# Convolution by a Winograd-like transform: order of work in the second unit, of the first unit's outer silu, and the engines of a few adds

## The chip, the cores and the metric

The kernel runs on one core of a Trainium2 chip. A core has a matrix engine (TensorE, PE in the profile), a vector engine (VectorE, DVE), a scalar engine (ScalarE, ACT), GpSimd (POOL), and an engine that mostly issues transfers (SyncE, SP). Each works through its own instructions in order and waits for the others on semaphores. TensorE writes only to PSUM, a memory of eight banks. The metric is device time in microseconds (us); lower is better.

## The reference

```python
y = sum(jnp.einsum('bsc,cd->bsd', xp[:, k:k + S, :], w[k]) for k in range(3))
y = (y - mean) * (g / sqrt(var + 1e-5)) + b
return silu(y)
```

This is a convolution of width 3 along the sequence (`xp` is `x` with one row of zeros at either end), a normalization by channel with given statistics, and a silu. Inputs and output are bfloat16; `x` is 2 x 2048 x 1024, `w` is 3 x 1024 x 1024.

## The kernel before, in words

The convolution is not made tap by tap. Six output rows at a time are computed from eight transformed inputs and eight transformed weights (a transform of Winograd's kind, with points 0, 1, -1, 2, -2, 1/2, -1/2 and infinity). There are 342 such blocks of six rows in each of the two batches.

The inputs are transformed on TensorE (`t_job`, L305 to L326): a matmul of windows of `x` with a small matrix, then a cast from PSUM to the tile `T_sb[bi]` on ScalarE or VectorE. Each cast goes to the engine that a small model of the engines' clocks, kept in Python while the program is written, says would end it first (`busy` and `ends` add to those clocks).

The weights are transformed for one block of 128 output channels (`dc`, 0 to 7) at a time. Taps 0 and 7 are the raw `w0` and `w2`. The six others come in three pairs, q = 0, 1, 2: a sum `e` (q = 0: `w0 + w2`; q = 1: `4 w2 + w0`; q = 2: `4 w0 + w2`), to which the middle tap (`w1`, or `2 w1` for q = 1 and 2) is added, or from which it is subtracted (`transform_w`, L184 to L190, on GpSimd: two instructions for a pair). The tiles are called `u0`, `u1`, `u2`. Where a sum needs four times a tap, VectorE does it in one instruction (L171), or another engine first writes the multiple to a scratch tile `w1x2` (two buffers) and GpSimd adds (L169, L249). There is one buffer for each of `e0`, `e1`, `e2`, and there are two for each of `u0`, `u1`, `u2`.

The main work goes by units: one block of channels and one batch, 15 whole units and a last one in two halves. Units take PSUM banks 0 to 3 and 4 to 7 in turn. A unit consists of eight products; a product (`product(q, j, ...)`, L351) is eight matmuls that add up over the input channels into one bank, q, of the unit. The order in a unit after the first (`run`, L465) is

```python
product(3,1); copy; product(0,3); copy; product(3,2); copy; product(0,4)
product(2,5); copy; product(2,6)   # then the previous unit's rest between
```

ScalarE copies a partial product away (`copy`, L366), and the next product adds into the same bank. VectorE combines banks and copies to the six output rows (`combine`, L376). Rows 0 and 5 lie in the unit's banks 0 and 3, rows 1 and 4 in banks 1 and 2, rows 2 and 3 in an SBUF tile `t1`. The two outer products, (0,0) with tap 0 for row 0 and (3,7) with tap 7 for row 5, are left for the next unit: `rest` (L457) returns pairs of a number and a function, and `run` calls those of number n at its point n (`behind(n)`; 1 to 4 stand behind the first four products, 5 behind the copy of (2,5), 6 at the end). In the usual order, `rest(between, 5, 6)`, the inner silus (`silu_inner`) and (3,7) with the silu of row 5 come at point 5, and (0,0) with the silu of row 0 at point 6. The silu (L380) reads PSUM or `t1` and writes `yT`. SyncE then transposes `yT` and stores it.

The first unit (`run_first`, L407) is different: its outer products come first and are copied to a tile `ends`, and the jobs that transform the second batch's inputs are put between its products. GpSimd adds `ends` to `t0` and `t2` (L435, L436), so nothing is left for later but the silus: `rest_first` (L450) puts the inner ones at point 5 and the outer ones, one instruction for both rows, at point 6 of the second unit. The weights of the second block of channels are made within the first two units by `prepare_second` (L232): `first` in the middle of the first unit, `times4` and the VectorE sum at its end, and `second` at point 1 of the second unit.

All instructions stay on each engine in the order in which the program issues them.

Of the kernel before, what the change touches and what calls it, by code (L numbers as in the profile page):

```python
# [9 lines left out]
ALU = mybir.AluOpType  # L10
# [5 lines left out]
P = 128  # L16
# [10 lines left out]
def kernel(  # L27
# [87 lines left out]
    def busy(e, size):  # L115
        clock[e] = ends(e, size)
# [115 lines left out]
    def prepare_second(dc):  # L232


        w0, w2 = raw[dc][:, 0], raw[dc][:, 2]
        g = spool.tile([P, CT, P], BF16, name="w1x2")

        def first():
            even_part(dc, 0, nc.gpsimd)
            transform_w(dc, 0, (0,))  # L240

        def times4():
            nc.scalar.mul(g, w2, 4.0)
            busy("act", CT * P)

        def second():
            double_w(dc, nc.scalar)
            sums[dc, 1] = epool.tile([P, CT, P], FP32, name="e1")
            nc.gpsimd.tensor_tensor(sums[dc, 1], g, w0, op=ALU.add)  # L249
            transform_w(dc, 1)  # L250
            transform_w(dc, 2)

        return first, times4, lambda: even_part(dc, 2, nc.vector), second

    prm = consts.tile([P, 4, DC], BF16, name="prm")
    scale = consts.tile([P, DC], FP32, name="scale")
# [78 lines left out]
    class Unit:  # L335
# [71 lines left out]
        def run_first(self, between, left, following):  # L407


            b0, b1, b2, b3 = self.bank  # L410
            sd = dpool.tile([P, 2, NB], FP32, name="sd")
            t0 = dpool.tile([P, 2, NB], FP32, name="t0")
            t2 = dpool.tile([P, 2, NB], FP32, name="t2")
# [12 lines left out]
            self.product(3, 2, True, between)  # L426
            self.copy(3, dst=sd[:, 0])
            self.combine(sd[:, 1], pa, 2.0, b3, ALU.subtract)
            self.product(0, 4, True, between)
            self.combine(b1, b0, -2.0, pb)  # L430
            for t, a in ((t0, -0.0125), (t2, -0.2), (t1, -0.05)):
                self.combine(t, self.low, a, sd)
            dc, (first, times4, third, second) = following
            first()
            nc.gpsimd.tensor_tensor(t0[:, 0], t0[:, 0], ends[:, 0], op=ALU.add)  # L435
            nc.gpsimd.tensor_tensor(t2[:, 1], t2[:, 1], ends[:, 1], op=ALU.add)  # L436
            transform_w(dc, 0, (1,))
            self.product(2, 5, False, between)
            pc = self.copy(2)
            between.rest()  # L440
            self.product(2, 6, True, between)
            self.combine(b3, b2, -0.5, pc)
            self.combine(self.low, self.high, -1.6, t0)
            self.combine(t1, self.high, -0.4, t1)
            self.combine(self.high, self.high, -0.1, t2)
            times4()
            third()
            self.second = second

        def rest_first(self):  # L450

            return [
                (1, self.second), (5, self.silu_inner),
                (6, lambda: self.silu(slice(0, R, R - 1), ps[:, self.b0:self.b0 + 4:3, self.lo:self.hi])),
            ]

        def rest(self, between, last=5, first=6):  # L457
# [4 lines left out]
                (first, lambda: self.first(between)),  # L462
            ]

        def run(self, between, also=(), prepare=None):  # L465
# [11 lines left out]
            t0 = dpool.tile([P, 2, NB], FP32, name="t0")[:, :, sl]  # L477
            t2 = dpool.tile([P, 2, NB], FP32, name="t2")[:, :, sl]
            self.y23 = t1 = ypool2.tile([P, 2, NB], FP32, name="t1")[:, :, sl]
            self.product(3, 1, False, between)  # L480
            pa = self.copy(3)
            behind(1)
            self.product(0, 3, False, between)
            pb = self.copy(0, by=4.0)
            behind(2)
            self.product(3, 2, True, between)
            self.copy(3, dst=sd[:, 0])
            self.combine(sd[:, 1], pa, 2.0, b3, ALU.subtract)
            behind(3)
            self.product(0, 4, True, between)  # L490
            behind(4)
            self.combine(b1, b0, -2.0, pb)
            for t, a in ((t0, -0.0125), (t1, -0.05), (t2, -0.2)):
                self.combine(t, self.low, a, sd)
            idle(dve_work)
            if prepare:
                prepare_w(prepare)
            self.product(2, 5, False, between)
            pc = self.copy(2)
            behind(5)  # L500
            self.product(2, 6, True, between)
            self.combine(b3, b2, -0.5, pc)
# [117 lines left out]
    for i, (dc, bi) in enumerate(seq[:-1]):  # L620
        unit = Unit(dc, bi, i % 2 * 4)
        if i == 0:
            unit.run_first(between, left[0], (1, prepare_second(1)))
# [67 lines left out]
```

## Time and profile before

| | |
|---|---|
| median of 3 runs | 190.01 us (190.00 to 190.02) |
| profiled execution | 190.22 us, span 188.5 us |
| TensorE busy | 177.0 us, 94% |
| VectorE busy | 154.2 us, 82% |
| GpSimd busy | 146.4 us, 78% |
| ScalarE busy | 111.0 us, 59% |

A row of a timeline has the start (us from the start of the span), the duration, the engine, the line of the kernel, the operation, what it writes and reads, the shapes, and how many instructions were merged into the row; in brackets stands how long the engine had been idle before and what released it. A row of waits has who waited for whom, then the total in us, the number of waits and the longest. A row of a group has the line, the shape and the count, then the busy time, the mean in ns and the idle time before. L359 is the matmul of the products, L370 and L372 are the copies, L377 is `combine`, L382 the silu. Durations of neighbouring instructions on one engine can overlap by about 0.1 us.

### The profile page before, as it was taken

The page shows a single profiled execution, that of the slowest core. Times are in us where ns is not written, and L with a number is a line of the kernel's source. Part 1 is how long each engine was busy: PE and PEld are TensorE (multiplying, and loading weights), DVE is VectorE, ACT ScalarE, POOL GpSimd, SP SyncE. Part 2 cuts the span into 40 slices and gives each one's busy share as a digit, 9 for nine tenths or more (in the row PEclk, how much of TensorE's full clock was granted, in tenths as well). Part 3 has the DMA queues.
Part 4 walks back from the last instruction along what each step waited for, and adds up shares of the span by engine and source line. Part 5 has one row for each costly group of instructions (what it writes and reads, how often), then busy time and mean ns, then how long its engine had stood idle before and what let it go on. Part 6 is the DMA issues. An engine that isn't in the chain of part 4 may idle for free.

```text
span 188.5 us, 3723 instructions
## 1 busy us (share of the span) xinstructions
PE 177.0 (94%) x1402; PEld 124.9 (66%) x1402; DVE 154.2 (82%) x213; ACT 111.0 (59%) x181; POOL 146.4 (78%) x87
## 2 busy tenths in 40 slices
PE   6769999998799999999999999999999999999981
PEld 2658688765466666666666666666666666669980
DVE  5548667899988999999877997799987996769781
ACT  3789698685547465456546563655455546364790
POOL 3468999979999779999999999899999972021022
PEclk9999999999999999999999999999999999999996
DMA  5999999057424839499669585996595766877835
GB/s 159 339 346 335 386 367 219 1 153 188 75 50 31 195 66 186 124 241 206 113 132 185 113 175 156 213 207 124 117 207 108 159 87 153 162 141 145 190 67 111
DMA packets 86958, 31.72 MB, mean 168 GB/s; under 512 B 73542, under 2 KB 82778, under 8 KB 86940
## 3 DMA queue, kind: packets, MB, share of 16 engines
q1 hardware_dynamic: 85820, 31.24, 72.4%
q10 hardware_dynamic: 864, 0.21, 0.5%
q8 instruction: 11, 0.18, 0.4%
q0 software_dynamic: 256, 0.03, 0.2%
q14 instruction: 7, 0.06, 0.1%
HBM read 14.82 MB, written 8.39 MB: 123 GB/s over the span
## 4 chain that ended last, share of the span: by engine, by line
PE 83%; DMA 5%; DVE 4%; ACT 3%; SPq 2%; issue 1%; DVEq 0%
PE ps L359 77%; PE ps L313 5%; DMA xw<-in_x_dram 5%; DVE T_sb L326 4%; SPq L125 2%; ACT yT L382 2%; ACT T_sb L324 1%; PE ps L521 1%; SPq L141 0%; DVEq L686 0%; ACT pc L370 0%; DVE sd L377 0%; DVE o L522 0%; DVEq L326 0%
## 5 line engine op out<-in xcount | busy, mean ns | idle before, releaser
L359 PE MATMUL ps<-T_sb,u 128*128 128x342 bf16 (+2 forms) x816 | 120.3, 299 | 1.7 <-ACT yT L382 1.2
L359 PEld LDWEIGHTS <-u 128*128 128x128 bf16 x816 | 76.7, 97 | 35.2 <-issue 2.1
L190 POOL TENSOR_TENSOR u<-e,w1x 128x1024 bf16<-128x1024 f32 x32 | 70.2, 2219 | 3.9 <-ACT sd L370 1.3
L359 PE MATMUL ps<-T_sb,wch 128*128 128x342 bf16 (+2 forms) x272 | 42.9, 299 | 0.5 <-ACT T_sb L324 0.5
L190 POOL TENSOR_TENSOR u<-e,wch 128x1024 bf16<-128x1024 f32 x16 | 38.7, 2435 | 1.8 <-DMA wch<-in_w_dram 1.2
L382 ACT ACTIVATE yT<-ps,beta,scale 128x342 bf16<-128x342 f32 (+4 forms) x49 | 33.6, 719 | 11.0 <-PE ps L359 10.9
L377 DVE SCALAR_TENSOR_TENSOR t<-ps,sd 128x684 f32<-128x684 f32 (+2 forms) x51 | 39.1, 821 | 0.6
L370 ACT COPY pc<-ps 128x342 f32<-128x342 f32 (+2 forms) x34 | 14.5, 427 | 33.8 <-PE ps L359 33.1
L359 PEld LDWEIGHTS <-wch 128*128 128x128 bf16 x272 | 25.6, 97 | 11.7 <-issue 0.7
L326 DVE CAST T_sb<-ps 128x1008 bf16<-128x1008 f32 (+2 forms) x20 | 22.1, 1121 | 11.8 <-PE ps L313 11.7
L324 ACT CAST T_sb<-ps 128x1008 bf16<-128x1008 f32 (+2 forms) x30 | 24.9, 866 | 7.2 <-PE ps L313 7.1
L377 DVE SCALAR_TENSOR_TENSOR ps<-ps,t 128x684 f32<-128x684 f32 (+2 forms) x34 | 28.3, 832 | 0.7
L313 PE MATMUL ps<-rm,xw 128*128 128x168 bf16 (+2 forms) x272 | 24.8, 233 | 3.1 <-DMA xw<-in_x_dram 2.6
L171 DVE SCALAR_TENSOR_TENSOR e<-wch 128x1024 f32<-128x1024 bf16 x13 | 26.7, 2051 | 0.0
L313 PEld LDWEIGHTS <-xw 128*128 128x128 bf16 (+2 forms) x272 | 20.1, 97 | 8.9 <-DMA xw<-in_x_dram 3.9
L377 DVE SCALAR_TENSOR_TENSOR ps<-ps,pc 128x342 f32<-128x342 f32 (+2 forms) x34 | 16.9, 496 | 7.8 <-PE ps L359 6.3
L169 POOL TENSOR_TENSOR e<-wch 128x1024 f32<-128x1024 bf16 x7 | 16.9, 2409 | 0.7 <-PE ps L359 0.7
L382 ACT ACTIVATE yT<-t,beta,scale 128x684 bf16<-128x684 f32 (+2 forms) x17 | 15.7, 926 | 0.0
L377 DVE SCALAR_TENSOR_TENSOR t<-ps,t 128x684 f32<-128x684 f32 (+2 forms) x17 | 13.9, 818 | 0.0
L377 DVE SCALAR_TENSOR_TENSOR sd<-pc,ps 128x342 f32<-128x342 f32 (+2 forms) x17 | 8.3, 486 | 6.8 <-ACT sd L370 6.7
L563 POOL DMA_DIRECT2D out_dram<-o x2 | 1.4, 712 | 15.6 <-DMA o<-yT 15.6
L370 ACT COPY sd<-ps 128x342 f32<-128x342 f32 (+2 forms) x17 | 7.3, 429 | 9.4 <-PE ps L359 9.2
(53 smaller groups left out, 57.9 us busy)
## 6 DMA issues: line engine op xcount, KB each, us to landing
xw<-in_x_dram SPq DMA_DIRECT2D x32, 256.0 KB
out_dram<-o SPq DMA_DIRECT2D x28, 192.0 KB
wch<-in_w_dram SPq DMA_DIRECT2D x9, 512.0 KB
out_dram<-o SPq DMA_DIRECT2D x14, 120.0 KB
wch<-in_w_dram SPq DMA_DIRECT2D x6, 256.0 KB
out_dram<-o SPq DMA_DIRECT2D x3, 128.0 KB
o<-yT SPq DMA_TRANSPOSE x15
out_dram<-o SPq DMA_DIRECT2D x12, 7.5 KB
```

The costliest lines, as they stand in the source:

```text
L125: nc.sync.dma_start(out=xw[0:hi - lo, :], in_=x[bi, lo:hi, :])
L169: eng.tensor_tensor(e, w0, w2, op=ALU.add)
L171: eng.scalar_tensor_tensor(out=e, in0=f, scalar=4.0, in1=h, op0=ALU.mult, op1=ALU.add)
L190: nc.gpsimd.tensor_tensor(wts[dc, q][:, i], sums[dc, q], o, op=(ALU.add, ALU.subtract)[i])
L313: nc.tensor.matmul(v[:, q, c], lhsT=xw[0:rows, (c0 + c) * P:(c0 + c + 1) * P], rhs=mat[0:rows, :, 0:n], start=True, stop=True,)
L324: nc.scalar.copy(dst, src)
L326: nc.vector.tensor_copy(dst, src)
L359: nc.tensor.matmul(self.bank[q], lhsT=lhsT, rhs=T_sb[self.bi][:, ct, j, nsl], start=not add and ct == 0, stop=ct == CT - 1, skip_group_che ...
L370: nc.scalar.copy(dst, self.bank[q])
L377: nc.vector.scalar_tensor_tensor(out=out, in0=in0, scalar=scalar, in1=in1, op0=ALU.mult, op1=op1)
L382: nc.scalar.activation(self.yT[:, rows, self.lo:self.hi], src, ACT.Silu, bias=beta[:, dc:dc + 1], scale=scale[:, dc:dc + 1])
L521: nc.tensor.transpose(v[:, a, q], self.yT[:, i, k * P:k * P + n], ident)
```

## The change

The change does six things.

- In the second unit alone (`alone`, i = 1), product (2,5) and its copy come ahead of product (0,4).
- The first unit's outer silu moves from point 6 to point 4 of the second unit, ahead of the inner silus, which stay at point 5.
- `ends` is added to `t0` and `t2` on VectorE, in one instruction over both: `t0` and `t2` become the halves of one tile `t02`. The instruction is also entered into the model of VectorE's clock. The two GpSimd adds go.
- All sums of the second block of channels are made on GpSimd: the q = 2 sum leaves VectorE, ScalarE writes 4 `w0` for it, and it is made behind the q = 1 pair.
- `prepare_second` is regrouped: both signs of `u0` are made one after the other; `4 w2` and the q = 1 sum come at the end of the first unit, `2 w1` and the `u1` pair at point 1 of the second, `4 w0`, the q = 2 sum and the `u2` pair at point 3.
- In the third unit (i = 2) the second unit's outer product (0,0) and its silu come at point 4 instead of point 6.

```diff
-        g = spool.tile([P, CT, P], BF16, name="w1x2")
+        def times4(tap):
+            t = spool.tile([P, CT, P], BF16, name="w1x2")
+            nc.scalar.mul(t, tap, 4.0)
+            busy("act", CT * P)
+            return t
+
+        def even(q, t, h):
+            sums[dc, q] = epool.tile([P, CT, P], FP32, name=f"e{q}")
+            nc.gpsimd.tensor_tensor(sums[dc, q], t, h, op=ALU.add)

         def first():
             even_part(dc, 0, nc.gpsimd)
-            transform_w(dc, 0, (0,))
-
-        def times4():
-            nc.scalar.mul(g, w2, 4.0)
-            busy("act", CT * P)
+            transform_w(dc, 0)

         def second():
+            even(1, times4(w2), w0)
+
+        def third():
             double_w(dc, nc.scalar)
-            sums[dc, 1] = epool.tile([P, CT, P], FP32, name="e1")
-            nc.gpsimd.tensor_tensor(sums[dc, 1], g, w0, op=ALU.add)
             transform_w(dc, 1)
+
+        def fourth():
+            even(2, times4(w0), w2)
             transform_w(dc, 2)

-        return first, times4, lambda: even_part(dc, 2, nc.vector), second
+        return first, second, third, fourth
...
-            for t, a in ((t0, -0.0125), (t2, -0.2), (t1, -0.05)):
-                self.combine(t, self.low, a, sd)
-            dc, (first, times4, third, second) = following
+            for d, a in ((t0, -0.0125), (t2, -0.2), (t1, -0.05)):
+                self.combine(d, self.low, a, sd)
+            nc.vector.tensor_tensor(t[:, 0::3], t[:, 0::3], ends, op=ALU.add)
+            busy("dve", 2 * NB)
+            first, second, third, fourth = following
             first()
-            nc.gpsimd.tensor_tensor(t0[:, 0], t0[:, 0], ends[:, 0], op=ALU.add)
-            nc.gpsimd.tensor_tensor(t2[:, 1], t2[:, 1], ends[:, 1], op=ALU.add)
-            transform_w(dc, 0, (1,))
             self.product(2, 5, False, between)
             pc = self.copy(2)
             between.rest()
...
-            times4()
-            third()
-            self.second = second
+            second()
+            self.prepare = third, fourth

         def rest_first(self):

             return [
-                (1, self.second), (5, self.silu_inner),
-                (6, lambda: self.silu(slice(0, R, R - 1), ps[:, self.b0:self.b0 + 4:3, self.lo:self.hi])),
+                (1, self.prepare[0]), (3, self.prepare[1]),
+                (4, lambda: self.silu(slice(0, R, R - 1), ps[:, self.b0:self.b0 + 4:3, self.lo:self.hi])),
+                (5, self.silu_inner),
             ]
...
             behind(3)
+            if alone:
+                self.product(2, 5, False, between)
+                pc = self.copy(2)
             self.product(0, 4, True, between)
             behind(4)
...
-            self.product(2, 5, False, between)
-            pc = self.copy(2)
+            if not alone:
+                self.product(2, 5, False, between)
+                pc = self.copy(2)
             behind(5)
...
-                prev.rest_first() if i == 1 else prev.rest(between, *((4, 5) if i >= len(seq) - 3 else (5, 6))),
+                prev.rest_first() if i == 1 else
+                prev.rest(between, *((4, 5) if i >= len(seq) - 3 else (5, 4) if i == 2 else (5, 6))),
                 2 if i == 2 else dc + 2 if bi == 1 and 0 < dc < DC - 2 else None,
+                i == 1,
             )
```

More of the change, by code (lines that the diff above doesn't have):

```diff
@@ L411, in run_first @@
             sd = dpool.tile([P, 2, NB], FP32, name="sd")
-            t0 = dpool.tile([P, 2, NB], FP32, name="t0")
-            t2 = dpool.tile([P, 2, NB], FP32, name="t2")
+            t = dpool.tile([P, 4, NB], FP32, name="t02")
+            t0, t2 = t[:, 0:2], t[:, 2:4]
             ends = dpool.tile([P, 2, NB], FP32, name="ends")
@@ L463, in rest, with run @@
             ]
-        def run(self, between, also=(), prepare=None):
+        def run(self, between, also=(), prepare=None, alone=False):
             def behind(n):
@@ L476, in run @@
             sd = dpool.tile([P, 2, NB], FP32, name="sd")[:, :, sl]
-            t0 = dpool.tile([P, 2, NB], FP32, name="t0")[:, :, sl]
-            t2 = dpool.tile([P, 2, NB], FP32, name="t2")[:, :, sl]
+            t02 = dpool.tile([P, 4, NB], FP32, name="t02")[:, :, sl]
+            t0, t2 = t02[:, 0:2], t02[:, 2:4]
             self.y23 = t1 = ypool2.tile([P, 2, NB], FP32, name="t1")[:, :, sl]
@@ L622 @@
         if i == 0:
-            unit.run_first(between, left[0], (1, prepare_second(1)))
+            unit.run_first(between, left[0], prepare_second(1))
         else:
```

## The prediction

> **What bounds the kernel now.** I read the page first (busy shares, chain), then TensorE's waits, then TensorE in order of time, and then the other engines in the few microseconds in which TensorE stands still.
>
> ```profile
> span 188.5 us, 3723 instructions
> PE 177.0 (94%) x1402; PEld 124.9 (66%) x1402; DVE 154.2 (82%) x213; ACT 111.0 (59%) x181; POOL 146.4 (78%) x87
> ...
> PE ps L359 <- ACT yT L382: 1.2, 1, 1.2
> ...
> PE ps L359 <- ACT pc L370: 0.5, 1, 0.5
> ```
>
> TensorE is busy 94% of the span. Two of its waits concern the products (L359): one for a silu, 1.2 us, and one for a copy, 0.5 us. The chain in order of time and TensorE's timeline say where they are:
>
> ```profile
> 48.83 126.89 PE ps L359 x888
> ...
> 38.64 7.17 PE L359 MATMUL ps<-T_sb,u 128*128 128x342 bf16 x48
> 46.35 1.32 PE L359 MATMUL ps<-T_sb,u 128*128 128x342 bf16 x8 [0.53 <-ACT pc L370]
> 48.83 5.97 PE L359 MATMUL ps<-T_sb,u 128*128 128x342 bf16 x40 [1.16 <-ACT yT L382]
> 54.63 1.32 PE L359 MATMUL ps<-T_sb,wch 128*128 128x342 bf16 x8
> ...
> 58.11 5.97 PE L359 MATMUL ps<-T_sb,u 128*128 128x342 bf16 x40
> ```
>
> The first row: from 48.83 on the chain is TensorE alone for 126.89 us. Whatever makes the third unit start earlier moves all that follows, as long as nothing new stops TensorE. Between 48.83 and 58.11 lie 8 products without a gap: 9.28/8 = 1.16 us for a product of 8 matmuls. From 38.64 to 48.83 are 7 products (unit 0's last and six of unit 1): 7 x 1.16 = 8.12 of 10.19 us. So 2.07 us are lost there, and this is all that the change can win.
>
> ```profile
> 40.05 1.07 ACT L243 ACTIVATE w1x<-wch 128x1024 bf16<-128x1024 bf16 x1
> ...
> 43.53 0.45 ACT L370 COPY sd<-ps 128x342 f32<-128x342 f32 x1 [0.25 <-ACT pc L372]
> 45.85 0.45 ACT L370 COPY pc<-ps 128x342 f32<-128x342 f32 x1 [1.88 <-PE ps L359]
> 46.19 0.96 ACT L382 ACTIVATE yT<-t,beta,scale 128x684 bf16<-128x684 f32 x1
> 47.05 1.72 ACT L382 ACTIVATE yT<-ps,beta,scale 128x684 bf16<-128x684 f32 x2
> ...
> 54.83 0.45 ACT L370 COPY pc<-ps 128x342 f32<-128x342 f32 x1 [1.83 <-PE ps L359]
> 55.17 0.96 ACT L382 ACTIVATE yT<-t,beta,scale 128x684 bf16<-128x684 f32 x1
> 56.03 1.44 ACT L382 ACTIVATE yT<-ps,beta,scale 128x684 bf16<-128x684 f32 x2
> ```
>
> ScalarE's rows up to 47.05 name both causes (those from 54.83 on, unit 2's, are for later). The copy of (2,5) starts at 45.85, when that product ends, and (2,6) adds into the same bank, so it starts at 46.35, after the copy. Then come three silus in a row (inner rows 0.96, and two in 1.72); the outer one, last, ends at 48.77. It reads banks 0 and 3, and unit 2 begins by writing bank 3: 48.83.
>
> **The change, part by part.** I write (q,j) for the product into bank q with tap j, and let TensorE run on at 1.16 us a product from 39.80, the end of unit 0's last product.
>
> Product (2,5) ahead of (0,4) in unit 1. New ends: (3,1) 40.96, (0,3) 42.12, (3,2) 43.28, (2,5) 44.44, (0,4) 45.60, (2,6) 46.76. The copy of (2,5) sees its product 0.20 after such an end (54.83 against 54.63 in unit 2), so at 44.64. But ScalarE now has the new times-4 of w0 ahead of it: after the sd copy, 43.98 less the 0.10 by which neighbours overlap, 1.07 as the row at 40.05: until 44.95. The copy runs 44.85 to 45.30. (2,6) wants it at 45.60: 0.3 us spare, the 0.53 wait goes. Its cover is product (0,4).
>
> Outer silu first, at point 4. It needs VectorE's last update of the high banks:
>
> ```profile
> 38.32 2.42 DVE L377 SCALAR_TENSOR_TENSOR t<-ps,sd 128x684 f32<-128x684 f32 x3
> 40.66 0.51 DVE L377 SCALAR_TENSOR_TENSOR ps<-ps,pc 128x342 f32<-128x342 f32 x1
> 41.28 0.88 DVE L377 SCALAR_TENSOR_TENSOR ps<-ps,t 128x684 f32<-128x684 f32 x1
> 42.07 0.86 DVE L377 SCALAR_TENSOR_TENSOR t<-ps,t 128x684 f32<-128x684 f32 x1
> 42.85 0.87 DVE L377 SCALAR_TENSOR_TENSOR ps<-ps,t 128x684 f32<-128x684 f32 x1
> 43.62 2.76 DVE L171 SCALAR_TENSOR_TENSOR e<-wch 128x1024 f32<-128x1024 bf16 x1
> 46.30 0.50 DVE L377 SCALAR_TENSOR_TENSOR sd<-pc,ps 128x342 f32<-128x342 f32 x1
> ...
> 51.72 0.87 DVE L377 SCALAR_TENSOR_TENSOR ps<-ps,t 128x684 f32<-128x684 f32 x1
> ```
>
> The update ends at 43.72 now. VectorE runs back to back from 38.32, so the added 684-wide add at 40.66 pushes it back by its whole length. No row shows that add; bounds: 0.78 (the step from one 684-wide row to the next, 42.07 to 42.85) and 1.84 (the only VectorE row with all operands in SBUF, 2.76 for 1024 elements beside GpSimd, times 684/1024). I take 0.86, the 684-wide row at 42.07, nearest in shape and type. The update ends at 44.58. ScalarE is free at 45.20, so the outer silu runs 45.20 to 46.11 (0.91, half of 1.72 and the overlap), and unit 2, which comes to bank 3 at 46.76, finds it free with 0.6 to spare. With 1.84 the silu would start at 45.56 and still be in time. The 1.16 wait goes too. The inner silus follow until about 48; their banks are wanted at 52.56.
>
> The page "SBUF — State Buffer" of the Trainium skill, section "Who interferes with whom", speaks against this add: a VectorE instruction with two SBUF inputs contends with a GpSimd instruction that reads SBUF, and the one that starts first keeps the port for its whole length. This trace agrees as far as the row at 43.62 goes: 2.76 us, beside GpSimd, for what takes 2051 ns in the mean of 13 (row below). By that rule GpSimd's e1 waits for the add, or the add for e1; the second is rival 2.
>
> Sums of the second block on GpSimd. The 2.76 at 43.62 leaves VectorE; the sd row behind it, 46.30, comes at about 44.5. With (0,4) ending at 45.60 unit 1's three t start at about 46.4 instead of 47.27, and its high update ends at 51.7 instead of 52.59; the first that asks for it is (3,7) of unit 1, now at 53.72. GpSimd before:
>
> ```profile
> 36.25 2.12 POOL L190 TENSOR_TENSOR u<-e,wch 128x1024 bf16<-128x1024 f32 x1
> 39.34 0.92 POOL L435 TENSOR_TENSOR t<-t,ends 128x342 f32<-128x342 f32 x1 [0.96 <-DVE t L377]
> 40.21 0.92 POOL L436 TENSOR_TENSOR t<-t,ends 128x342 f32<-128x342 f32 x1
> 41.08 2.13 POOL L190 TENSOR_TENSOR u<-e,wch 128x1024 bf16<-128x1024 f32 x1
> 43.17 2.13 POOL L249 TENSOR_TENSOR e<-w1x,wch 128x1024 f32<-128x1024 bf16 x1
> 45.38 9.26 POOL L190 TENSOR_TENSOR u<-e,w1x 128x1024 bf16<-128x1024 f32 x4
> 54.60 2.14 POOL L169 TENSOR_TENSOR e<-wch 128x1024 f32<-128x1024 bf16 x1
> ...
> 45.38 2.99 POOL L190 TENSOR_TENSOR u<-e,w1x 128x1024 bf16<-128x1024 f32 x1
> ...
> L171 DVE SCALAR_TENSOR_TENSOR e<-wch 128x1024 f32<-128x1024 bf16 x13 | 26.7, 2051 | 0.0
> ```
>
> Two adds of 0.92 and their wait of 0.96 leave GpSimd, one sum of 2.13 comes. Afterwards: second u0 38.45 to 40.57, e1 at 41.2 (its times-4 ends at 41.12), then at 2.15 each (41.08 to 43.17 to 45.38): u1 43.35 and 45.5, e2 47.65 (its times-4 was done at 44.95), u2 plus ready at 51.95, u2 minus at 54.1, against 54.60 for the end of this work now. Also, the slowest of the four u, 2.99, is the one beside VectorE's L171, which goes.
>
> "GPSIMD Engine Reference" of the Trainium skill, section 4.1, advises VectorE for elementwise adds, GpSimd being about twice as slow with two inputs. Here GpSimd takes 2.13 (row at 43.17) where VectorE took 2.76, so the measurement decides against it; were e2 4.1 instead, an estimate from twice the 2051 ns mean of L171, u2 plus would come 2 us later and the gain be about 0.1; rival 3 is that mechanism with rows of this trace.
>
> Third unit: first outer product (0,0) of unit 1 at point 4 instead of 6. Unit 2 from 46.76: (3,1) 47.92, (0,3) 49.08, (3,2) 50.24, (0,4) 51.40, (0,0) 52.56, (2,5) 53.72, (3,7) 54.88, (2,6) 56.04. (2,5) needs u2 plus from 52.56 on: ready 0.6 before. Were (0,0) still behind, it would be wanted at 51.40 and wait 0.55. (2,6) wants u2 minus at 54.88: ready. But the move has a price, which ScalarE's rows from 54.83 show. Behind (2,5) ScalarE makes the copy, the two inner silus and then the silu of row 5 (second of the pair at 56.03), which ends at 57.47, 2.84 after (2,5) ends at 54.63. That silu frees the bank into which unit 3 makes its first product. Now three products lie between (3.48 us); with (0,0) moved ahead only (3,7) and (2,6), 2.32 us. So unit 3 waits 2.84 + 0.05 (48.77 to 48.83, release) - 2.32 = 0.57 us. I see nothing that covers it: ScalarE's queue is the same and every step of it hangs on (2,5). Unit 3 starts at 53.72 + 2.89 = 56.61 instead of 58.11.
>
> Behind that the order is the old one, and weights for the next blocks are not near the edge: GpSimd itself waits there,
>
> ```profile
> 62.29 4.23 POOL L190 TENSOR_TENSOR u<-e,w1x 128x1024 bf16<-128x1024 f32 x2 [1.25 <-ACT sd L370]
> 67.74 4.22 POOL L190 TENSOR_TENSOR u<-e,w1x 128x1024 bf16<-128x1024 f32 x2 [1.23 <-DVE e L171]
> ```
>
> and these pairs end at 66.52 and 71.96, while unit 4 asks for them at 68.56 and 72.04 (67.40 plus 1.16 and 4 x 1.16), and both sides hang on the same units. Moving t0 and t2 into one tile costs nothing: VectorE alone uses them.
>
> Sum: -0.53, -1.16 and the issue gaps around them make -2.07; +0.57; net -1.50. The profiled execution took 190.22 us, 0.21 above the median of 190.01; I apply the difference to the median: 188.5.
>
> **The rivals.**
> 1. Full gain, no new wait: if row 5's silu goes faster or its bank is free sooner, 190.01 - 2.07 = 187.9. For it: TensorE has no wait in the 126.89 us now. Against: the 2.84 against 2.32 above.
> 2. The add doesn't get the port. It is due at 40.66, e1 at 41.2; should e1 (2.13) come first, the add ends at 44.2, the high update at 47.3, the outer silu at 48.2, and unit 2 waits 1.4 of the 2.07 won: 189.9, no real change. This decides once the add ends later than 42.7 (45.80, the last start of the silu that is in time, less the 3.06 from 40.66 to 43.72). Against: u0 is over at 40.57 and e1 can't start before 41.12.
> 3. Slower: GpSimd is late with u2 plus. Were its five operations from e1 on as long as the 2.99 row, it would be ready at 56.2, (2,5) would wait 3.6 us, and 190.01 - 1.50 + 3.6 = 192.1. It turns into a loss once u2 plus comes 1.50 after 52.56, that is once the five take over (54.06 - 41.2)/5 = 2.57 each. Against: only the one beside L171 took it, the others 2.13.
> 4. The waits stay where they are because the outer silu hangs on something else than the order: 190.0. The row of TensorE at 48.83 names that silu, so this has little.
>
> **How the numbers follow.** Forecast (both old waits gone, 0.57 new) 0.62; rival 1 0.14; rival 2 and parts of it 0.12; rival 3 0.08; rival 4 0.04. Range: down to 187.9 (rival 1), up to 189.4, which takes in about half of rival 2's loss; the forecast's own range is 188.2 to 188.8. A difference of 0.2% (0.4 us) is about what a measurement of this kernel can tell from none. Faster by more: 0.62 + 0.14 + most of rival 2 = 0.86; slower 0.08; within 0.06.
>
> **What the changed kernel's profile would show.** Right: no wait of TensorE for a copy in unit 1; unit 2 begins at about 46.8 without a wait; one wait of some 0.57 for a silu at about 56; the outer add on VectorE at 40.7, near 0.86; GpSimd's work for the second block over at about 54. It would be wrong if a wait for u2 (a weight load released by GpSimd) stood at 51 to 55, if the outer silu started later than 45.8, if TensorE had no wait at 56, or if later units showed waits that are not there now.

## The result and the profile after

| | before | changed |
|---|---|---|
| median on one chip, 6 runs each | 189.92 us (189.46 to 190.02) | 188.54 us (187.88 to 189.28) |
| ratio | | 0.9931, 95% interval 0.9907 to 0.9955 |
| profiled execution | 190.22 us, span 188.5 | 188.50 us, span 186.7 |

The forecast was 188.5 us in a range of 187.9 to 189.4. As in the prediction, unit 0 is the first unit, unit 1 the second, and so on. In the rows of the changed kernel the product is L368, the copies are L379 and L381, `combine` is L386, the silu L391, the new add L442. The first rows of its page:

```profile
span 186.7 us, 3721 instructions
PE 177.0 (95%) x1402; PEld 125.0 (67%) x1402; DVE 154.9 (83%) x213; ACT 111.9 (60%) x182; POOL 146.1 (78%) x86
```

and of TensorE's waits those that concern the products:

```profile
PE ps L368 <- ACT yT L391: 0.5, 1, 0.5
PE ps L368 <- ACT T_sb L333: 0.4, 1, 0.4
```

TensorE's busy time is the same 177.0 us. The wait for the copy (0.5) is gone from the list, and of the wait for a silu (1.2) a wait of 0.5 is left, which is another one. The wait for a cast (0.4) lies at the start and was 0.5 before. TensorE's timeline:

```profile
38.18 12.94 PE L368 MATMUL ps<-T_sb,u 128*128 128x342 bf16 x88
50.96 1.32 PE L368 MATMUL ps<-T_sb,wch 128*128 128x342 bf16 x8
52.12 1.33 PE L368 MATMUL ps<-T_sb,u 128*128 128x342 bf16 x8
53.28 1.32 PE L368 MATMUL ps<-T_sb,wch 128*128 128x342 bf16 x8
54.44 1.32 PE L368 MATMUL ps<-T_sb,u 128*128 128x342 bf16 x8
56.23 5.97 PE L368 MATMUL ps<-T_sb,u 128*128 128x342 bf16 x40 [0.46 <-ACT yT L391]
...
65.51 5.97 PE L368 MATMUL ps<-T_sb,u 128*128 128x342 bf16 x40
```

In place of three rows with two gaps stands one of 88 matmuls from 38.18 on: unit 0's last product, all six of the second unit and four of the third without a gap. The first row with `wch` is (0,0) of the second unit, now ahead of (2,5). At 56.23, the start of unit 3, stands the new wait. The last product is this row of the chain in order of time:

```profile
180.84 0.46 PE ps L368 x8
```

The whole stretch moved earlier by 0.46 us before the change begins (38.18 against 38.64), because the first transfers landed a little earlier in this execution. So I compare stretches that begin at unit 0's last product: to unit 3's start 56.23 - 38.18 = 18.05 against 58.11 - 38.64 = 19.47, that is 1.42 us less. To the start of unit 4 it is 27.33 against 28.76 (67.40), and from there to the last product 115.33 against 115.32 (182.72): nothing is given back. The medians differ by 1.38.

The timelines of VectorE, ScalarE and GpSimd around it:

```profile
40.20 0.86 DVE L442 TENSOR_TENSOR t<-t,ends 128x684 f32<-128x684 f32 x1
...
43.09 0.87 DVE L386 SCALAR_TENSOR_TENSOR ps<-ps,t 128x684 f32<-128x684 f32 x1
...
44.37 0.44 ACT L379 COPY pc<-ps 128x342 f32<-128x342 f32 x1
44.69 0.94 ACT L391 ACTIVATE yT<-ps,beta,scale 128x684 bf16<-128x684 f32 x1
45.51 0.96 ACT L391 ACTIVATE yT<-t,beta,scale 128x684 bf16<-128x684 f32 x1
46.36 0.93 ACT L391 ACTIVATE yT<-ps,beta,scale 128x684 bf16<-128x684 f32 x1
...
53.54 0.45 ACT L379 COPY pc<-ps 128x342 f32<-128x342 f32 x1 [0.58 <-PE ps L368]
53.88 0.96 ACT L391 ACTIVATE yT<-t,beta,scale 128x684 bf16<-128x684 f32 x1
54.74 1.44 ACT L391 ACTIVATE yT<-ps,beta,scale 128x684 bf16<-128x684 f32 x2
...
40.74 2.31 POOL L245 TENSOR_TENSOR e<-w1x,wch 128x1024 f32<-128x1024 bf16 x1 [0.67 <-ACT w1x L239]
43.13 4.23 POOL L190 TENSOR_TENSOR u<-e,w1x 128x1024 bf16<-128x1024 f32 x2
47.31 2.14 POOL L245 TENSOR_TENSOR e<-w1x,wch 128x1024 f32<-128x1024 bf16 x1
49.53 4.22 POOL L190 TENSOR_TENSOR u<-e,w1x 128x1024 bf16<-128x1024 f32 x2
```

The copy of (2,5) is done at 44.81, 0.3 us ahead of the end of (0,4); the outer silu follows at 44.69, first of the three. The second of the pair at 54.74 is the silu of row 5. It ends at 56.18, and TensorE goes on at 56.23.

### The profile page after: what moved, and what is told of

The parts are those of the page before. It is cut to its first block, busy times and chain, and to the rows that moved or that the text cites. A ratio compares the mean times of both kernels' runs of the same rounds, so it can differ in the third digit from the quotient of the medians.

```text
span 186.7 us, 3721 instructions
## 1 busy us (share of the span) xinstructions
PE 177.0 (95%) x1402; PEld 125.0 (67%) x1402; DVE 154.9 (83%) x213; ACT 111.9 (60%) x182; POOL 146.1 (78%) x86
## 4 chain that ended last, share of the span: by engine, by line
PE 83%; DMA 4%; DVE 4%; ACT 2%; SPq 2%; issue 1%; ACTq 0%; DVEq 0%
PE ps L368 77%; PE ps L322 5%; DVE T_sb L335 4%; DMA xw<-in_x_dram 3%; SPq L125 2%; DMA rows<-in_g_dram 1%; ACT yT L391 1%; ACT T_sb L333 1%; PE ps L534 1%; SPq L141 0%; ACTq L70 0%; DVEq L701 0%; ACT pc L379 0%; DVE sd L386 0%; DVE o L535 0%
## 5 line engine op out<-in xcount | busy, mean ns | idle before, releaser
L368 PE MATMUL ps<-T_sb,u 128*128 128x342 bf16 (+2 forms) x816 | 120.1, 299 | 0.5 <-ACT yT L391 0.5
L368 PEld LDWEIGHTS <-u 128*128 128x128 bf16 x816 | 76.7, 97 | 33.7 <-issue 0.7
L190 POOL TENSOR_TENSOR u<-e,w1x 128x1024 bf16<-128x1024 f32 x32 | 69.4, 2194 | 3.9 <-DVE e L171 2.5
L368 PE MATMUL ps<-T_sb,wch 128*128 128x342 bf16 (+2 forms) x272 | 43.0, 299 | 0.4 <-ACT T_sb L333 0.4
L391 ACT ACTIVATE yT<-ps,beta,scale 128x342 bf16<-128x342 f32 (+4 forms) x49 | 33.8, 721 | 11.9 <-PE ps L368 11.9
L386 DVE SCALAR_TENSOR_TENSOR t<-ps,sd 128x684 f32<-128x684 f32 (+2 forms) x51 | 39.1, 822 | 0.6
L368 PEld LDWEIGHTS <-wch 128*128 128x128 bf16 x272 | 25.6, 97 | 11.7 <-issue 0.7
L379 ACT COPY pc<-ps 128x342 f32<-128x342 f32 (+2 forms) x34 | 14.5, 427 | 30.1 <-PE ps L368 30.0
L386 DVE SCALAR_TENSOR_TENSOR ps<-ps,t 128x684 f32<-128x684 f32 (+2 forms) x34 | 28.3, 832 | 0.6
L171 DVE SCALAR_TENSOR_TENSOR e<-wch 128x1024 f32<-128x1024 bf16 x12 | 27.2, 2263 | 0.0
L386 DVE SCALAR_TENSOR_TENSOR ps<-ps,pc 128x342 f32<-128x342 f32 (+2 forms) x34 | 16.8, 496 | 8.6 <-PE ps L368 7.5
L391 ACT ACTIVATE yT<-t,beta,scale 128x684 bf16<-128x684 f32 (+2 forms) x17 | 15.7, 926 | 0.0
L386 DVE SCALAR_TENSOR_TENSOR t<-ps,t 128x684 f32<-128x684 f32 (+2 forms) x17 | 13.9, 818 | 0.0
L379 ACT COPY sd<-ps 128x342 f32<-128x342 f32 (+2 forms) x17 | 7.3, 429 | 9.7 <-PE ps L368 8.8
L381 ACT ACTIVATE pc<-ps 128x342 f32<-128x342 f32 (+2 forms) x17 | 7.5, 440 | 9.1 <-PE ps L368 6.8
```

What stands on the lines that cost most here:

```text
L171: eng.scalar_tensor_tensor(out=e, in0=f, scalar=4.0, in1=h, op0=ALU.mult, op1=ALU.add)
L190: nc.gpsimd.tensor_tensor(wts[dc, q][:, i], sums[dc, q], o, op=(ALU.add, ALU.subtract)[i])
L368: nc.tensor.matmul(self.bank[q], lhsT=lhsT, rhs=T_sb[self.bi][:, ct, j, nsl], start=not add and ct == 0, stop=ct == CT - 1, skip_group_che ...
L379: nc.scalar.copy(dst, self.bank[q])
L381: nc.scalar.mul(dst, self.bank[q], by)
L386: nc.vector.scalar_tensor_tensor(out=out, in0=in0, scalar=scalar, in1=in1, op0=ALU.mult, op1=op1)
```

## The experiments

All kernels were compared with the kernel before on the same chip. Medians of one kernel differ by some tenths from one set of runs to the next (188.54 and 188.87 for the changed one), and the start of unit 0's last product, which hangs on the first transfers, lies anywhere from 37.97 to 39.05 us in these profiles; the place of a loss is read better from two stretches of the profiled execution: A, from the start of unit 0's last product to the start of unit 4, and B, from there to the start of TensorE's last product.

| | A | B | A + B | median us | ratio to before (95%) |
|---|---|---|---|---|---|
| before | 28.76 | 115.32 | 144.08 | 189.86 to 190.12 | 1 |
| changed | 27.33 | 115.33 | 142.66 | 188.54 | 0.9931 (0.9907 to 0.9955) |
| e1 row 5 first | 26.71 | 115.76 | 142.47 | 188.84 | 0.9934 (0.9908 to 0.9960) |
| e2 usual third unit | 27.47 | 115.33 | 142.80 | 188.93 | 0.9951 (0.9932 to 0.9971) |
| e3 not ahead | 28.07 | 115.32 | 143.39 | 189.22 | 0.9961 (0.9947 to 0.9975) |
| e4 order only | 27.83 | 115.32 | 143.15 | 189.02 | 0.9964 (0.9940 to 0.9988) |
| e5 outer silu late | 28.35 | 115.32 | 143.67 | 190.06 | 1.0009 (0.9996 to 1.0022) |
| e6 adds on GpSimd | 28.85 | 115.48 | 144.33 | 189.41 | 0.9977 (0.9961 to 0.9993) |
| e7 sum on VectorE | 27.42 | 115.32 | 142.74 | 189.27 | 0.9968 (0.9947 to 0.9989) |
| e8 order only, row 5 first | 27.44 | 115.65 | 143.09 | 188.85 | 0.9949 (0.9930 to 0.9969) |
| e9 row 5 first, late sum | 27.32 | 115.33 | 142.65 | 187.97 | 0.9898 (0.9886 to 0.9911) |
| e10 changed, again | 27.33 | 115.32 | 142.65 | 188.87 | 0.9942 (0.9922 to 0.9963) |
| e11 as e9, sum on VectorE | 26.81 | 115.32 | 142.13 | 188.44 | 0.9920 (0.9907 to 0.9933) |
| e12 as e9, add in PSUM | 26.71 | 115.32 | 142.03 | 188.17 | 0.9897 (0.9880 to 0.9913) |

e1 to e4 ran side by side, so did e5 to e8 and e9 to e11, and e12 ran alone.

### One part undone: (2,5) ahead, and the outer silu first

```diff
-                i == 1,          # e3: the last argument of unit.run
+                False,
```

> The changed kernel without the first part: (2,5) behind (0,4) in the second unit as before. Theory: ScalarE has the outer silu in hand when (2,5) ends and copies after it, so (2,6) waits about 0.75 us for the copy and nothing later takes it back: near 189.3. Rival: the loss is hidden because unit 2 would otherwise wait for bank 3 or for u2: 188.5.

Measured: A is 0.74 longer than in the changed kernel, with these rows (timelines of TensorE and ScalarE):

```profile
46.07 5.96 PE L368 MATMUL ps<-T_sb,u 128*128 128x342 bf16 x40 [0.53 <-ACT pc L379]
...
44.59 0.90 ACT L391 ACTIVATE yT<-ps,beta,scale 128x684 bf16<-128x684 f32 x1
45.58 0.45 ACT L379 COPY pc<-ps 128x342 f32<-128x342 f32 x1
```

The theory's amount stands, and the rival falls: nothing later takes it back. Its reason holds only in small part. (2,5) ends at 45.32 here (six products of 1.16 after 38.36), and a copy sees its product some 0.20 later, so the copy could not have started before 45.52; it starts at 45.58, so the silu, which ends at 45.49, delays it by 0.06 at most. The rest is lost because (2,6) stands directly behind (2,5) and needs its copy. In the kernel before, where ScalarE was idle at that point, 0.75 were lost as well (46.35 against 38.64 and six products).

```diff
-                (4, lambda: self.silu(slice(0, R, R - 1), ...)),      # e5
-                (5, self.silu_inner),
+                (5, self.silu_inner),
+                (6, lambda: self.silu(slice(0, R, R - 1), ...)),
```

> The changed kernel with the first unit's outer silu behind the inner ones again (point 6). Theory: the copy of (2,5) is early now, so the three silus run from about 45.2 to 47.8 on the clock of the trace before; unit 2 waits 1.1 us for bank 3 instead of 0: near 189.6. Rival: the wait is shorter because the time is given back at the third unit, where row 5's silu sets the start of unit 3 all the same: 188.5 to 189.0.

TensorE's timeline of e5, at the start of unit 2:

```profile
47.32 4.81 PE L368 MATMUL ps<-T_sb,u 128*128 128x342 bf16 x32 [0.86 <-ACT yT L391]
```

Measured: A 1.02 longer, against 1.1. So undoing one half of the order costs most of what the kernel before lost at that place (0.74 of 0.75, and 1.02 of 1.32), and the two together carry the gain. The median of this kernel, 190.06, is more above the changed one than 1.02 (by 1.19 to 1.52); its profiled execution, 189.38 us, is the fastest of its twelve runs, and of the excess I can't show a cause.

### The third unit: what the move of (0,0) costs and saves

```diff
-                ... else (5, 4) if i == 2 else (5, 6))),              # e2
+                ... else (5, 6))),
```

> The changed kernel with the usual order in the third unit: (0,0) of the second unit back at point 6. Theory: the wait for row 5's silu goes, but (2,5) is asked for 1.16 us earlier and waits for u2 plus, which ends at 51.64 in the changed kernel's trace while (2,5) would be due at 50.94: a wait of 0.7 released by GpSimd, time within 0.2 us of the changed kernel. Rival: the weights are early enough, no wait at all, 187.9.

TensorE's timeline of e2, at (2,5) of unit 2:

```profile
51.73 1.34 PE L368 MATMUL ps<-T_sb,u 128*128 128x342 bf16 x8 [0.59 <-POOL u L190]
```

Measured: A 0.14 longer. The wait for row 5 is gone and one for GpSimd's u2 has come, as the theory has it. The move of (0,0) in this unit swaps one wait for another of nearly the same size.

```diff
+        def rest_row5(self, between):                                 # e1, for i == 2
+            return [
+                (4, lambda: self.first(between)), (5, lambda: self.silu(slice(2, 4), self.y23)),
+                (5, lambda: self.last(between)), (5, lambda: self.silu(slice(1, 5, 3), self.mid)),
+            ]
```

> The changed kernel, but in the third unit the second unit's silu of row 5 stands between the two inner silus (order: rows 2 and 3, row 5, rows 1 and 4). Theory: the one wait left in TensorE's products (0.46 us shown as wait, 0.63 between 54.44 + 1.16 and 56.23) is there only because row 5 stands last in ScalarE's queue; its bank should be free about 2.0 us after the end of (2,5), and TensorE comes to it at 2.32, so no wait at unit 3's start and about 0.6 us less than the changed kernel: near 187.9, ratio to before about 0.990. Rival: the third unit's stretch is bound by something else (GpSimd's u2, VectorE's updates), and the wait only moves: time as the changed kernel, 188.5.

Measured: A is 0.62 shorter, which the theory said, but B is 0.43 longer. TensorE waits at a place where it did not wait before, and VectorE's rows ahead of it show why (timelines of e1):

```profile
81.09 1.32 PE L368 MATMUL ps<-T_sb,wch 128*128 128x342 bf16 x8 [0.22 <-DVE ps L386]
...
76.08 2.06 DVE L171 SCALAR_TENSOR_TENSOR e<-wch 128x1024 f32<-128x1024 bf16 x1
...
80.17 0.87 DVE L386 SCALAR_TENSOR_TENSOR ps<-ps,t 128x684 f32<-128x684 f32 x1
```

The same update and the same product in the changed kernel (its timelines of VectorE and TensorE):

```profile
79.45 0.87 DVE L386 SCALAR_TENSOR_TENSOR ps<-ps,t 128x684 f32<-128x684 f32 x1
...
80.61 1.32 PE L368 MATMUL ps<-T_sb,wch 128*128 128x342 bf16 x8
```

The product at 81.09, (3,7) of unit 4, adds to a bank that VectorE's update at 80.17 to 81.04 must have left. VectorE has made four weight sums (L171) of 2.06 to 2.64 us within 20 us, and its update ends 0.33 after the product is due (80.71, five products of 1.16 after 74.91, the start of unit 5). In the changed kernel the same update ended at 80.32 with the product due at 80.61: it had 0.29 to spare, which the 0.62 used up. So the theory holds for the place and fails for the total: most of the gain is lost to another engine's backlog 25 us on. The medians, 188.84 here and 188.54 and 188.87 for the changed kernel, show no gain at all.

### The moves between engines

```diff
+            if alone:                         # e4: the kernel before, with these three changes alone
+                self.product(2, 5, False, between); pc = self.copy(2)
...
+                (4, lambda: self.silu(slice(0, R, R - 1), ...)), (5, self.silu_inner),
...
+                prev.rest(between, ... (5, 4) if i == 2 else (5, 6) ...)
```

> The kernel before with the three changes of order alone ((2,5) ahead, outer silu first, (0,0) at point 4 of the third unit); the adds stay on GpSimd and the second block's q = 2 sum on VectorE. Theory A (the moves between engines matter): u2 is late or VectorE's updates are late, a wait of 0.3 us or more at (0,0), (2,5) or (2,6) of the third unit, 188.9 or more. Theory B (order alone brings it): by the trace of before u2 plus is ready at about 52.5 and asked for at 52.56, VectorE's low update at 51.04 and asked for at 51.40, so all is just in time and the time is that of the changed kernel, 188.5 within 0.2. I lean to B.

The timelines of e4, with the lines of the kernel before (TensorE at the second product of unit 2, VectorE, GpSimd):

```profile
47.79 3.65 PE L359 MATMUL ps<-T_sb,u 128*128 128x342 bf16 x24 [0.33 <-POOL u L190]
...
42.99 2.76 DVE L171 SCALAR_TENSOR_TENSOR e<-wch 128x1024 f32<-128x1024 bf16 x1
...
44.74 3.00 POOL L190 TENSOR_TENSOR u<-e,w1x 128x1024 bf16<-128x1024 f32 x1
```

Measured: stretch A is 0.50 longer than in the changed kernel. Theory B falls, though the wait is not where theory A looked: it is for u1 plus, the first of GpSimd's two u1, at the third unit's second product. That instruction starts at 44.74 and takes 3.00, beside VectorE's sum that runs to 45.75, so it ends at 47.74. Of the 1.43 that the change gains in stretch A, order alone brings 0.93.

```diff
-            nc.vector.tensor_tensor(t[:, 0::3], t[:, 0::3], ends, op=ALU.add)     # e6
-            busy("dve", 2 * NB)
...
             first()
+            nc.gpsimd.tensor_tensor(t[:, 0::3], t[:, 0::3], ends, op=ALU.add)
```

> The changed kernel with the adds of the outer products on GpSimd, as one 684-wide instruction behind both u0. Theory: GpSimd gets some 1.8 us more ahead of e1 (twice 0.92), less the 0.65 for which it waits there anyway, so u2 plus comes 1.2 us later, and (2,5) of the third unit waits 0.6 for it: near 189.1. Rival: VectorE, which must wait for the add before it can update the low banks, makes the outer silu late instead: a wait at unit 2's start, also some tenths.

The timelines of e6 (TensorE at (2,6) of unit 1, GpSimd, ScalarE):

```profile
46.54 5.97 PE L368 MATMUL ps<-T_sb,u 128*128 128x342 bf16 x40 [1.13 <-ACT pc L379]
...
42.93 2.14 POOL L245 TENSOR_TENSOR e<-w1x,wch 128x1024 f32<-128x1024 bf16 x1
...
45.10 1.06 ACT L239 ACTIVATE w1x<-wch 128x1024 bf16<-128x1024 bf16 x1 [1.49 <-POOL e L245]
46.06 0.43 ACT L379 COPY pc<-ps 128x342 f32<-128x342 f32 x1
```

A is 1.52 longer. The wait that the theory names is there, but only with 0.23 (TensorE comes to (2,5) of the third unit at 53.50 and starts it at 53.73). The other 1.3 are in neither theory: they are lost at (2,6) of unit 1, by a wait of ScalarE. The times-4 of w0 (45.10) goes into one of two scratch buffers, the one that e1 on GpSimd reads until 45.07; the copy of (2,5) stands behind it in ScalarE's queue, and (2,6) waits for the copy. A part of it is not the edit's: in this execution GpSimd waited 2.50 us for a load of the first weights, against 1.30 in the changed kernel, and all of its work came later with it (u0 ended at 41.38 instead of 40.07). How much of the 1.52 that makes is not shown. The ratios to the kernel before (0.9977 against 0.9931 and 0.9942) speak for a loss of some 0.7 to 0.9.

```diff
             even(1, times4(w2), w0)
+            even_part(dc, 2, nc.vector)        # e7
...
-            even(2, times4(w0), w2)
             transform_w(dc, 2)
```

> The changed kernel with the second block's q = 2 sum on VectorE at the end of the first unit, as before, and no times-4 of w0 on ScalarE. Theory: VectorE's updates of the second unit come 2.5 us later; the low update ends at about 52.0 where (0,0) is due at 51.4 (clock of the trace before), so TensorE waits 0.6 for VectorE there, and GpSimd's u2 is 2 us early: near 189.1. Rival: that wait is taken out of the one at unit 3's start: 188.5.

Measured: A 0.09 longer, where 0.6 was expected. VectorE's low update and (0,0), timelines of VectorE and TensorE:

```profile
50.98 0.88 DVE L386 SCALAR_TENSOR_TENSOR ps<-ps,t 128x684 f32<-128x684 f32 x1
...
51.91 1.32 PE L368 MATMUL ps<-T_sb,wch 128*128 128x342 bf16 x8
```

The update ends at 51.86, and (0,0), due at 51.81 (eleven products of 1.16 after 39.05), starts at 51.91. The expectation was wrong in the delay: the update came 1.3 us later than in the changed kernel, not 2.5, because there VectorE stands idle for 0.98 us, up to 45.35, and the sum fills that. The 1.3 are about what (0,0) had to spare (49.68, the end of the update there, against 50.96). So the move of the q = 2 sum to GpSimd is worth next to nothing here; the median, 189.27 of runs from 188.43 to 190.53, is too scattered to tell more.

> The kernel before with the three changes of order alone and the silu of row 5 between the inner ones in the third unit. If order alone does it, this loses no wait at unit 3's start and lies near 187.9, as the changed kernel with the same order of silus does; if the moves between engines matter, it stays 0.3 us or more behind that one.

This is e4 with e1's order of the silus. A is 27.44 and B 115.65, together 0.62 more than in e1. Some 0.2 of it are not the edit's: here too the first weights came late (GpSimd waited 2.47 for them), and TensorE lost 0.73 at u1 plus where it lost 0.50 in e4. The rest says that the moves between engines matter, with or without the wait at unit 3. It rests on the stretches alone; the medians of e1 and e8, 188.84 and 188.85, are alike.

### A better version

```diff
-            idle(dve_work)                    # e9, with e1's order of the silus
+            if not sum_late:                  # sum_late is i == 4
+                idle(dve_work)
...
             self.combine(self.high, self.high, -0.1, t2)
+            if sum_late:
+                idle(dve_work)
```

> Row 5's silu between the inner ones in the third unit, and in the fifth unit (i = 4) VectorE's sum for the weights moves from the middle of the unit to its end. The first alone took the stretch from the first unit's last product to the fifth unit's start from 27.33 to 26.71 us but lost 0.43 again later, with TensorE waiting for VectorE at 81.09. Theory: VectorE is one sum (2.06 us at 76.08) too busy ahead of that point, and GpSimd, busy with u1 until 84.3, does not need the sum before; moved behind the unit's updates it costs nothing: stretch 26.7, no wait for VectorE, from the fifth unit's start to the last product 115.3 as in the changed kernel; 0.6 us less than that kernel. Rival: VectorE has no slack in the units after either, and the wait only comes a unit later: the time of the first alone.

> The changed kernel once more, beside the two others on the same chip: 188.5 within 0.4, stretch 27.3 and 115.3, whatever the first transfers do.

> As the first of these three, but with the second block's q = 2 sum on VectorE as before the change. If the move of that sum to GpSimd matters at all, it is here, where the third unit has no other wait to hide behind: (0,0) came 0.09 us late when the sum was on VectorE, and VectorE's backlog of 0.8 us goes on into the following units. Theory: 0.1 to 0.3 us behind the first of the three. Rival: equal, so that the sum's move brings nothing.

B is 115.33 in e9 and 115.32 in e11: with the sum behind the updates, VectorE's wait at unit 4 is gone, and the gain of e1 stays. e9's median is 187.97, against 188.87 for the changed kernel beside it (e10, runs from 188.07 to 189.91; its stretches are those of the first profile, 27.33 and 115.32). But e9's profiled execution has A = 27.32, not 26.71, and its trace shows why (timelines of GpSimd, VectorE, ScalarE, TensorE):

```profile
20.22 2.13 POOL L190 TENSOR_TENSOR u<-e,wch 128x1024 bf16<-128x1024 f32 x1 [2.57 <-DMA wch<-in_w_dram]
...
39.24 2.13 POOL L190 TENSOR_TENSOR u<-e,wch 128x1024 bf16<-128x1024 f32 x1
41.33 2.75 POOL L245 TENSOR_TENSOR e<-w1x,wch 128x1024 f32<-128x1024 bf16 x1
...
40.23 1.87 DVE L442 TENSOR_TENSOR t<-t,ends 128x684 f32<-128x684 f32 x1
...
44.12 1.06 ACT L239 ACTIVATE w1x<-wch 128x1024 bf16<-128x1024 bf16 x1 [0.58 <-POOL e L245]
...
45.56 5.97 PE L368 MATMUL ps<-T_sb,u 128*128 128x342 bf16 x40 [0.22 <-ACT pc L379]
```

GpSimd waited 2.57 for the first weights instead of 1.30, so its second u0 runs until 41.37. VectorE's add wants to start at 40.23 and takes 1.87 instead of 0.86: it ends 0.73 after u0 does, as if it had stood still until then. e1, which starts beside it, takes 2.75 instead of 2.13; ScalarE's times-4 waits for e1's buffer, the copy behind it comes late, and TensorE loses 0.39 (0.22 of it shown as the wait), and another 0.2 for u2 later. Nothing of this is in the two profiles of the changed kernel, where the weights came early. Of the nine profiles that have this add, seven show 0.86; in e3, where GpSimd waited 1.94 for the weights, it took 1.23, at no cost to TensorE.

e11, with the sum on VectorE, has A = 26.81. Up to the end of that stretch it differs from e1 (26.71) in the sum's place alone, so the sum's move to GpSimd brings a tenth in the best order. No times-4 of w0 stands on ScalarE there. The medians of e9 and e11 differ by more, 0.47; the stretches don't show from what.

```diff
-            nc.vector.tensor_tensor(t[:, 0::3], t[:, 0::3], ends, op=ALU.add)     # e12, on top of e9
-            busy("dve", 2 * NB)
...
             self.combine(self.high, self.high, -0.1, t2)
+            outer = ps[:, self.b0:self.b0 + 4:3, self.lo:self.hi]
+            self.combine(outer, outer, 1.0, ends)
```

> Row 5's silu between the inner ones, the late sum in the fifth unit, and the first unit's outer products added on VectorE in PSUM (banks 0 and 3 with one SBUF input, behind the last update) instead of in SBUF ahead of it. In two of the ten profiles so far the first weights' last third landed 1.3 us later, GpSimd's u0 then ran past the start of the add, and the add took 1.87 instead of 0.86 us in the one of the two that had it on VectorE, with waits of 0.45 us for TensorE behind it. Theory (a port shared by VectorE's two-SBUF-input instructions and GpSimd): the add in PSUM takes near 0.87 whenever the weights come, and e1 on GpSimd 2.13 and not 2.31; the outer silu still starts in time (VectorE's chain ends when it did); from the first unit's last product to the last product 142.05 us with no wait of TensorE in the products, and a median of 187.9 or less. Rival: the add's length had to do with something else, or VectorE's chain makes the outer silu late: a wait at the third unit's start, 188.2 or more.

The timelines of VectorE and GpSimd of e12:

```profile
43.01 0.88 DVE L386 SCALAR_TENSOR_TENSOR ps<-ps,ends 128x684 f32<-128x684 f32 x1
...
40.53 2.13 POOL L245 TENSOR_TENSOR e<-w1x,wch 128x1024 f32<-128x1024 bf16 x1 [0.61 <-ACT w1x L239]
```

The add takes 0.88 and e1 2.13; A + B is 142.03, with no wait of TensorE in the products from unit 0's last one on, 2.05 less than before. That is the whole of what the prediction said was to be won. The median is 188.17, 0.27 above what was expected, with the profiled execution at 187.61. In this execution the weights landed early, so that the add in PSUM is also better when they come late was not seen; by e9's rows it should be (an estimate: e1 would end 0.62 earlier, at 43.46, and the copy at 44.9, where (2,6) is due at 45.17). The expectation counted two late landings in ten profiles; in the thirteen profiles taken before this run there are three, e6, e8 and e9, with waits of GpSimd from 2.47 to 2.57, and e3 lies between. By ratio e12 and e9 are alike (0.9897 and 0.9898), and both are ahead of the changed kernel's 0.9942 and 0.9931.

## Why the prediction was right

Clock times of the prediction are those of the trace before; the changed kernel's trace is 0.46 earlier.

- (2,5) ahead: the copy was to end at 45.30, 0.3 before it is needed. It ends at 44.81 + 0.46 = 45.27, and (2,6) does not wait. Right; e3 gives the part back when it is undone.
- The outer silu first: the add was to start at 40.66 and take 0.86, the silu to start at 45.20. Measured 40.20 + 0.46 = 40.66, 0.86, and 44.69 + 0.46 = 45.15. Unit 2 starts without a wait. Right; e5 gives it back when it is undone.
- GpSimd's chain: u2 plus was to be ready at 51.95. The first of the pair at 49.53 takes half of it and ends at 51.64, 52.10 on the old clock. The 0.15 is mostly e1, which took 2.31 instead of 2.13 beside the add.
- The new wait at unit 3: 0.57 forecast. TensorE lost 56.23 - (54.44 + 1.16) = 0.63. Its place, its releaser and its size were those of the sum, and e1 shows that the order of the silus alone makes it.
- The trade of the third unit, 0.55 against 0.57, came out as 0.14 in favour of the move (e2).
- The net, 1.50, was 1.42 in the profile and 1.38 in the medians. The difference is made by the new wait (0.06) and hundredths. That the first median, 188.54, met the 188.5 to 0.04 is luck: the second was 188.87, with runs from 188.07 to 189.91, and a gain of 1.1 by its ratio. The stretch from unit 0's last product, 1.42 against 1.50, is what bears the forecast out.
- One reading was wrong. The prediction let VectorE's 2.76 for the q = 2 sum against GpSimd's 2.13 decide that the sum is better on GpSimd. The sum starts at 43.62, and e1 on GpSimd runs until 45.30, so 1.68 of the 2.76 are spent standing behind it; from there the sum takes 1.08. The row did not show VectorE to be slower, and the move that rested on it brings 0.1 (e7, e11).

Of the rivals, the first (no new wait) falls with the wait itself, the third (GpSimd late) and the fourth with a trace in which TensorE runs from 38.18 to 54.44 without a gap. The second, the add that does not get the port, did not happen in the changed kernel's profiled execution, but it happened in e9's, with 1.87 for the add. There it started before the port was free, and what it cost TensorE was not the outer silu, as I had written, but the copy behind ScalarE's times-4. "u0 is over at 40.57" took the landing of the first weights as given, and that step of the argument failed: it moves by 1.3 us from one execution to the next. Rule and row agree in e9: the section "Who interferes with whom" of "SBUF — State Buffer" (the Trainium skill) says that the later of the two stands still until the first is through, and the add ended 0.73 after u0 did. In e3 it met the last 0.49 of u0, took 1.23, and again ended 0.73 after it. The size of the effect in the medians of the changed kernel was not measured by itself.

What the prediction had not seen is how the parts share the gain: order alone has 0.93 of the 1.43 (e4), and the q = 2 sum on GpSimd, which the change made a point of, 0.1 (e7, e11). The rest, some 0.4, is with the adds and the regrouping: e7 differs from e4 by these two alone, 27.42 against 27.83. They were not parted further; e6, which undoes the adds, had the late weights.

## What to carry to other kernels

Where the chain is one engine without a gap, add up its gaps first: 10.19 us less seven products of 1.16 gave the whole possible gain, and e12 got just that. A wait taken away moves on to the next engine in line with the least slack, so write down the slack of each (here 0.3 us of VectorE, 25 us later) before counting on the gain. And where two engines meet at a shared resource by luck of timing, look at more than one execution: one trace in which they missed each other does not show the cost.

## What the hardware showed that I had not expected

VectorE's sums with two SBUF inputs (L171) take from 1.22 to 3.00 us in one and the same trace, always 128 x 1024 elements. In the changed kernel (the row of the line's instructions, minimum, median and maximum in ns):

```profile
L171 DVE SCALAR_TENSOR_TENSOR e<-wch x12: 1216/2348/2995, 58.8 to 147.6; 128x1024 f32<-128x1024 bf16 x12
```

In e9 the sum that was moved took 1.25 where it had taken 2.06 in e1 (the row at 76.08 above). GpSimd's rows beside it say why (timelines of GpSimd in e1, then of VectorE and GpSimd in e9):

```profile
74.92 2.14 POOL L190 TENSOR_TENSOR u<-e,wch 128x1024 bf16<-128x1024 f32 x1
77.02 3.12 POOL L190 TENSOR_TENSOR u<-e,wch 128x1024 bf16<-128x1024 f32 x1
...
79.29 1.25 DVE L171 SCALAR_TENSOR_TENSOR e<-wch 128x1024 f32<-128x1024 bf16 x1
...
77.33 2.14 POOL L190 TENSOR_TENSOR u<-e,wch 128x1024 bf16<-128x1024 f32 x1
79.42 3.12 POOL L190 TENSOR_TENSOR u<-e,w1x 128x1024 bf16<-128x1024 f32 x1
```

In e1 GpSimd's running instruction ends at 77.06, 0.98 after the sum's start, and in e9 at 79.47, 0.18 after it; from there the sum takes about 1.08 in both. In the changed kernel eleven of the twelve sums end 1.08 after the GpSimd instruction in which they started, and the twelfth, which met none, took 1.22. GpSimd's next instruction takes 3.12 instead of 2.13 in e1 as well as in e9. So such a sum costs VectorE 1.1 us and what is left of GpSimd's running instruction, and GpSimd another 1.0 if its next instruction is ready; that the sum was short in e9 is a matter of where it happened to start. A mean of 2.05 us over all of them, as I used it, is no duration of anything.
